# Another written order for the pairs of a decode step's attention, with another kept unit

## Chip, cores, metric

One core of one Trainium2 chip. The metric is the device time of one launch in microseconds, the median of several runs; a profiled execution of the kernel shows where that time is spent.

## What is computed

Two layers, each an attention block over a cache and a gated feed-forward block, for four batches with one new token each. Both layers use the same weights and the same cache.

```python
B, D = 4, 512; Hq, Hkv, Sk, Dh = 32, 8, 4096, 128
def A(x):                                   # attention over the cache
    q = (x @ wq) as [B, Hq, 1, Dh]; k, v = caches, each repeated 4 times over heads
    p = softmax(q @ k.T * Dh ** -0.5)
    return (p @ v) @ wo
def G(x):                                   # F = 1792
    return (sigmoid(x @ w_gate) * (x @ w_up)) @ w_down
for layer in range(2):
    x = x + A(layernorm(x))
    x = x + G(layernorm(x))
```

All tensors are bf16. One batch and one of the 8 heads of the cache make a *unit*: its K and its V are 4096 x 128 values each, 1 MiB. 64 units for two layers would be 128 MiB.

## The kernel before, in words

**Units and pairs.** Work goes in *pairs* of neighbouring units of one batch and layer. `ORDER` lists them as three digits: layer, batch, pair (pair `k` holds units `2k` and `2k+1`). Pair 132 is layer 1, batch 3, units 4 and 5; the text writes a unit as (layer, batch, unit). Pairs are counted from 0 in the order of the list, so the last is pair 31.

**Slots and kept units.** SBUF holds 12 slots of 1 MiB, and four more once the query weights (`wq`) are used for the last time (`yield_wq`). Each slot takes one unit's K or V. `KEPT` names, for each batch, the units whose K (before the stroke) or V (after it) stays in its slot from layer 0 to layer 1 and is not loaded again: 27 in all, in both versions. The others are loaded once in each layer.

**The stream.** `LOADS` is the order in which SyncE issues all transfers: `k` and `v` take the next unit of `ORDER` that must be loaded, `o`, `g`, `u`, `d` are parts of the weights `wo`, `w_gate`, `w_up`, `w_down`. The text counts its letters from 0 and calls that the *place* of a transfer. After every step, `pump()` issues as many as there are free slots, and never out of order: a `k` or `v` without a slot holds back all that follow. A slot comes free when its user is through: two K at the pair's `z`, a V at its unit's second `a`. SyncE does nothing else, so a transfer is queued behind the wait of the one ahead of it. The very last V is cut in two transfers of 512 KiB.

**The program.** `PROGRAM` is one letter per step; each step issues its instructions to the engines, which work through them in order and wait for each other by semaphores. For the n-th pair:
- `t`, `T`: the transpose of half or the whole of one K in its slot, on VectorE (L1018); only for K that are loaded in that layer
- `b`: the pair's queries into blocks, on GpSimd (L732, four copies)
- `s`, `z`: first and second half of the scores, 8 matmuls each (L1035)
- `m`, `p`, `n`: maximum on VectorE (L1053), spread by TensorE (L1061), bias on VectorE (L1072)
- `e`: exponential on ScalarE (L1084)
- `P`, `C`, `D`: the probabilities turned by TensorE (L1106, 9 matmuls) and copied back in two parts of four copies, mostly on ScalarE (L1158)
- `h`, `r`, `i`: the row sums, on GpSimd, TensorE (L1172) and VectorE (L1184)
- `a`: a quarter of the pair's value products, 16 matmuls (L1204); two `a` for each unit
- `o`: normalise on VectorE (L1235); `N` the same for one unit at the very end
- `w`: output rows of a pair whose units are ready (L1260 or L1300), or nothing if none are. In layer 1 a unit is ready only when all four batches are through with it.
- `f`, `F`, `l`: the layer-0 output of a batch turned back into columns
- `x`: sums of the output weights, on ScalarE
- `.`: the next of the 17 steps of a batch's *pass* (`pass_steps`): feed-forward of layer 0 and the queries of layer 1 for that batch. Among them are the gate and up products (L837, L862; L875 combines them on VectorE), their turn (L887, L897), the down product (L957, L972), the layernorm (L494, L581 on TensorE) and the four query products (L908), after which L940, L706 and L717 bring the queries to where `b` reads them. Pairs of layer 1 of a batch can start only after its pass. The last of batch 3's query products is what frees the four `wq` slots.

`s12` in the text is the step `s` of pair 12, `a50` the two `a` steps of the 50th unit in the order of the list (units 2g and 2g+1 are those of pair g).

After the last `a`, the feed-forward block of layer 1 for all four batches and the output follow (L1300 to L1532).

Of the kernel before, what the change touches and what calls it, by code (L numbers as in the profile page):

```python
# [120 lines left out]

KEPT = ["012345/23", "0145/45", "167/067", "014567/7"]
ORDER = """
000 003 002 001 011 013 101 010 012 100 102 021 022 020 023 112 110 111 031 103 123 032 030 033 120
122 121 131 113 132 133 130
"""
LOADS = """
kvkkkkkkvo koovoovkko ovovgvkkvg uuddvvvkkv kkvvkkvvvk kvvvkkvvkk vvvvvvkkvk kvvvkkvvkv kvkkvvkkvv  # L130
kvvkkkvkkk kvkvvvvvvv vvvvv
"""
PROGRAM = """
szmbpTneTh szTTmprPnbDCwiaa swewazaohtPbtrmptCnDtwiaewaa szTbhraPTw
szwmpwonemCiDharpnabawaoPwiDeCTawtPaftFaal sowzmh.p.Dw..r.n.ehwiCP.r...aa..w.awao.Ci.Daa..b
szwTtmptabneaohx sPrzmwpiCDnTaeaaaPobChDriTaax szaawmwbpnx sehzPotrmpibx szCnwDeaatbT
smzpwbafnPahFlCDoeriwma.paT.hTrw..n..Paa seh.zC.Doi.aa.aram..w.oPb.wiDTT.pwCaa
snzm.aaehorPCpnTTwwebD.Pi shaazraaCmpnob sDzeibaaPh
szmrapaoCwnDewbmiahfFaPpaalCorDinweaaaTwTahPCroDi. szm.wbapnTTeaww..hPr..aa
swzboCDia.a.mpn.aaeho.rPiT..DTC...aa sz.a.bmap snezPChwmptrDnoitaabTePwaaohr  # L140
sCizDmaapaanteotwPhrwCiaTbDa szmawpnehbTaroiPTwCDaa szmaapbnoehwfrTPC
szwiDmaaFpanablePhoriCtwtD.aaT..T. sz..maa.pT.b.n soe.zmh..T...wPpCri..abTDna szTePaTbhaw
smrowpziCbnaDameph snPzabeCaorm sDipaPaahDnazrCwbeomwPhCip
sawnaerazamhoDPiwaCraapnaoiwaDaaeaPohCrDiwaaaNwa
"""


def bass_interleave_layers__gqa_block_cached__glu_gated_glu__decode_kernel(
# [147 lines left out]
    pos = {t: i for i, t in enumerate(seq)}  # L296
    hold = [dict(zip("kv", ([int(c) for c in part] for part in text.split("/")))) for text in KEPT]

# [1285 lines left out]
```

## Time and profile before

| | |
|---|---|
| median of 3 runs | 315.44 us (314.36 to 315.73) |
| profiled execution: its time, its span | 315.29 us, 313.2 us |
| TensorE matmuls busy | 228.6 us (73% of the span) |
| VectorE, ScalarE, GpSimd busy | 177.7, 106.7, 40.4 us |
| moved by DMA | 120.45 MB, 385 GB/s in the mean |
| mean granted TensorE clock | 0.719 |

The span runs from the first to the last instruction of the kernel; the execution's own time lies 2.1 us above it. Busy time is the union of an engine's instructions. The profile also holds the chain of work that ended last, followed back from the last instruction (each piece with its start and length in us, and either the engine and line that worked or the DMA that was waited for), and the landing of each transfer, which is when the last of the 16 DMA engines has finished its share.

### The profile page before, as it was taken

To read this page: it belongs to the slowest core of one execution; us is meant where nothing else is said; L and a number is where in the kernel's file an instruction comes from. 1 tells how busy PE (TensorE), PEld (TensorE's weight loads), DVE (VectorE), ACT (ScalarE), POOL (GpSimd) and SP (SyncE) were. 2 spreads that over 40 slices of the span, in tenths; PEclk is the share of its full clock that TensorE was granted. 3 is DMA by queue.
4 is the path that set the end of the run, shared out by engine and by line. 5 is a ranking of instruction groups with operands and counts; after the bars stand their busy time and mean duration, and the time that the engine had idled before them with its cause. 6 is when DMAs were issued, how large, how long until landed. Compare 5 with 4: busy or idle time off the path is not lost.

```text
span 313.2 us, 10155 instructions
## 1 busy us (share of the span) xinstructions
PE 228.6 (73%) x4306; PEld 140.0 (45%) x4306; DVE 177.7 (57%) x396; ACT 106.7 (34%) x351; POOL 40.4 (13%) x205
## 2 busy tenths in 40 slices
PE   1213264562888979798789899978676888799876
PEld 1211042232454354655445747345443543446765
DVE  6344916715424568567742675856655787832243
ACT  2001033043123366343425533344334312457420
POOL 0002110110000213201212011020121010232000
PEclk9999999999999976875655557555555576555555
DMA  7999999999999999999999999999999999999900
GB/s 289 420 426 422 399 375 414 384 422 417 404 417 421 395 374 425 422 422 416 419 392 370 421 425 416 420 421 421 416 419 358 398 365 365 421 426 419 396 31 5
DMA packets 20788, 120.45 MB, mean 385 GB/s; under 512 B 1924, under 2 KB 6024, under 8 KB 7688
## 3 DMA queue, kind: packets, MB, share of 16 engines
q1 hardware_dynamic: 20720, 119.81, 94.2%
q8 instruction: 34, 0.56, 0.7%
q14 instruction: 10, 0.08, 0.1%
q10 hardware_dynamic: 24, 0.01, 0.0%
HBM read 119.80 MB, written 0.00 MB: 383 GB/s over the span
## 4 chain that ended last, share of the span: by engine, by line
PE 37%; DMA 27%; SPq 13%; DVE 11%; ACT 5%; issue 4%; POOL 1%; DVEq 0%; ACTq 0%; POOLq 0%
DMA slot<-in_A_k_cache_dram 13%; PE S_ps L1035 12%; DMA slot<-in_A_v_cache_dram 11%; PE O_ps L1204 9%; SPq L369 8%; DVE slot L1018 7%; SPq L349 5%; PE PT L1106 4%; ACT pT L1158 3%; DMA wq<-in_A_v_cache_dram 3%; PE M_ps L908 2%; PE O_ps L1300 2%; POOL qz L732 1%; ACT pe L1084 1%; DVE small L1053 1%
## 5 line engine op out<-in xcount | busy, mean ns | idle before, releaser
L1018 DVE STREAM_TRANSPOSE slot<-slot 128x2048 f32<-128x2048 f32 (+1 forms) x53 | 103.9, 1973 | 18.9 <-DMA slot<-in_A_k_cache_dram 18.8
L1158 ACT ACTIVATE pT<-PT 32x128 bf16<-32x128 f32 x232 | 62.0, 267 | 69.3 <-PE PT L1106 38.0
L1204 PE MATMUL O_ps<-pT,slot 128*128 128x4 bf16 x1760 | 57.0, 166 | 24.6 <-ACT pT L1158 13.7
L1204 PEld LDWEIGHTS O_ps<-pT,slot 128*128 128x128 bf16 x1760 | 52.9, 103 | 46.0 <-ACT pT L1158 22.6
L1035 PE MATMUL S_ps<-slot,qz 128*16 128x512 bf16 x512 | 59.1, 590 | 15.2 <-DVE slot L1018 8.7
L732 POOL COPY qz<-qs 32x32 bf16<-32x32 bf16 x128 | 26.0, 203 | 125.9 <-PE S_ps L1035 72.5
L1084 ACT ACTIVATE pe<-S_ps,small 128x512 bf16<-128x512 f32 x32 | 22.0, 687 | 57.8 <-DVE small L1072 25.6
L1053 DVE TENSOR_REDUCE small<-S_ps 128x1 bf16<-128x512 f32 x32 | 21.9, 686 | 31.6 <-PE S_ps L1035 31.6
L1106 PE MATMUL PT<-ident_bf,pe 128*128 128x64 bf16 (+1 forms) x288 | 27.7, 235 | 2.7 <-ACT pT L1158 1.3
L1106 PEld LDWEIGHTS PT<-ident_bf,pe 128*128 128x128 bf16 (+1 forms) x288 | 20.4, 123 | 15.9 <-ACT pe L1084 4.3
L1035 PEld LDWEIGHTS S_ps<-slot,qz 128*16 128x16 bf16 x512 | 10.8, 101 | 30.0 <-issue 11.0
L1235 DVE TENSOR_TENSOR oT<-O_ps,small 128x8 bf16<-128x8 f32 (+1 forms) x32 | 5.4, 168 | 26.8 <-PE O_ps L1204 25.5
L1117 POOL CAST small<-small 128x1 bf16<-128x1 f32 x32 | 5.9, 186 | 88.7 <-ACT pe L1084 68.9
L1072 DVE CUSTOM_DVE_ANT_0 O_ps<-O_ps,small 128x64 f32<-128x64 f32 x32 | 9.1, 283 | 14.2 <-PE O_ps L1061 12.2
L908 PE MATMUL M_ps<-wq,small 128*1 128x512 bf16 x128 | 14.1, 605 | 0.0
L1260 PE MATMUL AC<-wo,oT 128*1 128x512 bf16 x96 | 12.5, 599 | 1.4 <-issue 0.8
L1061 PE MATMUL O_ps<-valid_p,small 128*128 128x64 bf16 x32 | 7.2, 225 | 7.5 <-DVE small L1053 6.9
L717 ACT ACTIVATE qs<-M_ps 128x128 bf16<-128x128 f32 x8 | 1.9, 280 | 25.0 <-PE M_ps L706 24.9
L1061 PEld LDWEIGHTS O_ps<-valid_p,small 128*128 128x128 bf16 x32 | 3.3, 103 | 14.5 <-DVE small L1053 11.6
L1300 PE MATMUL O_ps<-oT,wo 128*128 128x1 bf16 (+1 forms) x256 | 8.3, 166 | 1.9 <-issue 1.2
L1172 PE MATMUL O_ps<-small 128*128 128x8 bf16 x62 | 6.4, 174 | 4.2 <-POOL small L1120 3.7
L1172 PEld LDWEIGHTS O_ps<-small 128*128 128x128 bf16 x62 | 4.3, 110 | 11.0 <-issue 4.2
(129 smaller groups left out, 198.3 us busy)
## 6 DMA issues: line engine op xcount, KB each, us to landing
slot<-in_A_v_cache_dram SPq DMA_DIRECT2D x49, 1024.0 KB, 12.2
slot<-in_A_k_cache_dram SPq DMA_DIRECT2D x45, 1024.0 KB, 11.4
wq<-in_A_v_cache_dram SPq DMA_DIRECT2D x6, 1024.0 KB, 13.2
wq<-in_A_wq_dram SPq DMA_DIRECT2D x2, 2048.0 KB, 10.0
wo<-in_A_wo_dram SPq DMA_DIRECT2D x8, 512.0 KB, 14.9
wg<-in_B_w_gate_dram SPq DMA_DIRECT2D x2, 896.0 KB, 15.7
wu<-in_B_w_up_dram SPq DMA_DIRECT2D x2, 896.0 KB, 20.9
wd<-in_B_w_down_dram SPq DMA_DIRECT2D x1, 1024.0 KB, 23.9
```

The lines of the kernel that those rows point to most:

```text
L349: S.dma("sp", (lambda dst, src: lambda e: e.dma_start(dst, src))(dst, src), f"wo{n}" if kind == "wo" else kind, writes=[f"{kind}{n}"])
L369: "sp", (lambda dst, frm: lambda e: e.dma_start(dst, frm))(dst, frm), sem, writes=[key], deps=deps
L732: (lambda a, ps: lambda e: e.tensor_copy(qz_sb[ps, :, :, a, :], qs_sb[b][ps, :, u * REP:(u + 2) * REP].rearrange("p t (u r) -> p u t r", r ...
L908: (lambda k, st: lambda e: e.matmul(M_ps[h][32 * st:32 * st + 1, :], lhsT=xc_bf[:, k, 0:1], rhs=wv[:, k, h, :, st, :], start=(k == 0), sto ...
L1018: dve(lambda e: e.transpose(kf, kf), writes=[f"s{st}"])
L1035: (lambda t, b2, e_, c, r0, ul: lambda e: e.matmul(S_ps[p][r0:r0 + 4 * REP, :], lhsT=qz_sb[:, ul, t, :, :].rearrange("p a r -> p (a r)"), ...
L1053: dve(lambda e: e.tensor_reduce(rm_bf, S_ps[p][:, :], AX.X, ALU.max), reads=[f"S{p}"], writes=["rmb"])
L1084: lambda e: e.activation(pe_sb.rearrange("p j m -> p (j m)"), S_ps[p][:, :], ACTF.Exp, bias=nm_sb, scale=exp_scale, accum_out=sm_sb,),
L1106: (lambda q0, q1, c0, m0, m1, a0, a1: lambda e: e.matmul(PT[q0:q1, c0:c0 + 16 * (a1 - a0)], lhsT=pe_flat[:, m0:m1], rhs=valid_bf[:, :, 4 * ...
L1158: (lambda dst, frm: lambda e: e.activation(dst, frm, ACTF.Copy))(dst, frm),
L1204: (lambda n, x, c, j: lambda e: e.matmul(bank[:, ul * REP:(ul + 1) * REP], lhsT=vv[:, x * JG + c * 4 + j, :], rhs=pT[:, x % 2, j, x // 2, ...
L1300: (lambda c, r: lambda e: e.matmul(out_w[:, c * nb:(c + 1) * nb], lhsT=wo_sb[:, us[0] * REP + r, cols(c)], rhs=oT_sb[:, us[0] * REP + r, c ...
```

## The change

The four strings are replaced; no function is touched.

- `KEPT`: of batch 3, K of units 1, 4, 5, 6, 7 and V of units 6, 7 stay for layer 1, instead of K of units 0, 1, 4, 5, 6, 7 and V of unit 7. Batches 0 to 2 keep the same.
- `ORDER`: layer 0 begins with pair 003 instead of 000, and pairs within the middle change places. The last eight pairs were 120, 122, 121, 131, 113, 132, 133, 130 and need 2, 4, 4, 4, 4, 2, 1, 2 transfers; now they are 120, 121, 111, 133, 131, 130, 122, 132 and need 2, 4, 4, 0, 4, 3, 4, 2. The last unit to be loaded is (1,3,5) instead of (1,3,1).
- `LOADS` and `PROGRAM` follow that order, with the same steps at partly other places.

```diff
-KEPT = ["012345/23", "0145/45", "167/067", "014567/7"]
+KEPT = ["012345/23", "0145/45", "167/067", "14567/67"]
 ORDER = """
-000 003 002 001 011 013 101 010 012 100 102 021 022 020 023 112 110 111 031 103 123 032 030 033 120
-122 121 131 113 132 133 130
+003 002 000 001 011 013 101 010 012 102 100 021 022 020 023 112 110 103 031 113 123 030 032 033 120
+121 111 133 131 130 122 132
 """
 LOADS = """
-kvkkkkkkvo koovoovkko ovovgvkkvg uuddvvvkkv kkvvkkvvvk kvvvkkvvkk vvvvvvkkvk kvvvkkvvkv kvkkvvkkvv
-kvvkkkvkkk kvkvvvvvvv vvvvv
+kkvvkkokok kkkvvokoog oovovkkvvg uuddvvvkkv kkvvkkvvvv kkvkvkvvkk vvvvvvkkvv kkvkvkvvkk vvkkvvkkvv
+kvvkkkvkvv kvkkvkkvvv vvvvv
 """
 PROGRAM = """
...
-swzboCDia.a.mpn.aaeho.rPiT..DTC...aa sz.a.bmap snezPChwmptrDnoitaabTePwaaohr
-sCizDmaapaanteotwPhrwCiaTbDa szmawpnehbTaroiPTwCDaa szmaapbnoehwfrTPC
-szwiDmaaFpanablePhoriCtwtD.aaT..T. sz..maa.pT.b.n soe.zmh..T...wPpCri..abTDna szTePaTbhaw
-smrowpziCbnaDameph snPzabeCaorm sDipaPaahDnazrCwbeomwPhCip
-sawnaerazamhoDPiwaCraapnaoiwaDaaeaPohCrDiwaaaNwa
...
+sDiFlCzampaawbnaeoPthwrit.wCaDTa...Tw swzmb..aap..nTe.oPC shzri.Dwaawm.....pnw.waaTehr.bPCot
+sitzDabmapne sTzhaabmrpowPwniDC sezaaThwwTaarPDbCmo spzneimhbwapPwDanaa
+sCrozeihmPDapCnaaaeowrPiDwChwaaaaawroaiaNwa
 """
```

The text names three steps of these strings often: `a50` and `a51` (in the program before, the value products of units (1,2,4) and (1,2,5); after, of (1,2,2) and (1,2,3)), and the last query product of batch 3, the fifteenth `.` of that batch.

More of the change, by code (lines that the diff above doesn't have):

```diff
@@ L114 @@
 NSLOT = 12
-KEPT = ["012345/23", "0145/45", "167/067", "014567/7"]
+KEPT = ["012345/23", "0145/45", "167/067", "14567/67"]
 ORDER = """
-000 003 002 001 011 013 101 010 012 100 102 021 022 020 023 112 110 111 031 103 123 032 030 033 120
-122 121 131 113 132 133 130
+003 002 000 001 011 013 101 010 012 102 100 021 022 020 023 112 110 103 031 113 123 030 032 033 120
+121 111 133 131 130 122 132
 """
 LOADS = """
-kvkkkkkkvo koovoovkko ovovgvkkvg uuddvvvkkv kkvvkkvvvk kvvvkkvvkk vvvvvvkkvk kvvvkkvvkv kvkkvvkkvv
-kvvkkkvkkk kvkvvvvvvv vvvvv
+kkvvkkokok kkkvvokoog oovovkkvvg uuddvvvkkv kkvvkkvvvv kkvkvkvvkk vvvvvvkkvv kkvkvkvvkk vvkkvvkkvv
+kvvkkkvkvv kvkkvkkvvv vvvvv
 """
 PROGRAM = """
[L134 to L139, printed above, removed]
-swzboCDia.a.mpn.aaeho.rPiT..DTC...aa sz.a.bmap snezPChwmptrDnoitaabTePwaaohr
-sCizDmaapaanteotwPhrwCiaTbDa szmawpnehbTaroiPTwCDaa szmaapbnoehwfrTPC
-szwiDmaaFpanablePhoriCtwtD.aaT..T. sz..maa.pT.b.n soe.zmh..T...wPpCri..abTDna szTePaTbhaw
-smrowpziCbnaDameph snPzabeCaorm sDipaPaahDnazrCwbeomwPhCip
-sawnaerazamhoDPiwaCraapnaoiwaDaaeaPohCrDiwaaaNwa
+sTzmpnbewT szhmPrbTpwTnCi sewzDhampraaaoPTnibeCDTa saaaPhzbTmT sCropnezwwmiaDaTaawpwPbnhworehCDTw
+siPaazmrapfaFlonweC..wD.ih...P.r...aa...aao.Ci.Daa..bTw szmpnaTbehaoPtCrx sizmDapantaaebPThDowrwCx
+siaazbaampx snwezthPmworbpCtx snizwTabwDmewafw sFpnzaawhmoPCDrilw.aa.aaehTo..PrT.bDp.in
+szCe.aaw.ht.Pt.aaoCmrD.iTb..p.naea szam.pahorTnPD.TCwbe.Pihr saazaambCp sznoDebimaa
+szhPbaparnCowwDmiaaePfhaaCDrpneoiaFhaTaarlTPwoi sCzm.Dwaap.anTa..eT.b.hoP
+sCrzbwiamD.ap.neT.aa.ohPT..wD.r sziC..wama.apw.bwta snteTzhPrCbo
+simDzbpanaamaehpPrnDoiCaeahPraaTTCoi szmpanDaebharPawowwCiDaTwaT szbmaapneowhrPTf
+sDiFlCzampaawbnaeoPthwrit.wCaDTa...Tw swzmb..aap..nTe.oPC shzri.Dwaawm.....pnw.waaTehr.bPCot
+sitzDabmapne sTzhaabmrpowPwniDC sezaaThwwTaarPDbCmo spzneimhbwapPwDanaa
+sCrozeihmPDapCnaaaeowrPiDwChwaaaaawroaiaNwa
 """
```

## Prediction

> **What bounds the kernel now.** I read the page first (slices and chain), then the chain of waits in order of time for its last third, then stretches of 2 us, the timeline and SyncE's issues for the end. The slices:
>
> ```profile
> PE   1213264562888979798789899978676888799876
> DMA  7999999999999999999999999999999999999900
> GB/s 289 420 426 422 399 375 414 384 422 417 404 417 421 395 374 425 422 422 416 419 392 370 421 425 416 420 421 421 416 419 358 398 365 365 421 426 419 396 31 5
> ```
>
> The transfers run from the start to slice 38 at 420 GB/s where they are fed, and TensorE is nearly full from slice 13 on. The stream sets the pace; where its rate dips (slices 31 to 34, 235 to 266 us) it is TensorE that is late in freeing slots. From one transfer to the next the trace's landings stand 2.48 us apart (1 MiB, 423 GB/s). The last stage in the chain:
>
> ```profile
> 260.38 3.37 PE M_ps L908 x30
> 263.76 8.07 DMA wq<-in_A_v_cache_dram
> 271.88 1.01 PE O_ps L1204 x32
> ...
> 295.08 0.73 issue
> 295.81 1.85 PE O_ps L1204 x64
> 297.66 0.81 PE PT L1106 x9
> ...
> 299.15 1.16 issue
> 300.31 0.48 PE O_ps L1300 x12
> 300.79 0.87 PE O_ps L1204 x32
> ```
>
> The chain leaves the stream for good at 271.88: the value product of unit (1,2,5) waits for a transfer that could start only at 263.76, when batch 3's last query product (L908) gave the four wq slots free. After it every piece is TensorE's, or a short wait between engines. The stream itself ends earlier:
>
> ```profile
> 296.00:298.00 2.00, 2.00 (x69) 1.95 (x66) 0.18 (x1) 0.00 (x0) 0.00 (x0) 0.50 0.75 297
> 298.00:300.00 2.00, 1.15 (x29) 0.94 (x26) 1.37 (x5) 1.38 (x5) 0.00 (x0) 0.50 0.16 59
> 300.00:302.00 2.00, 1.70 (x60) 1.68 (x60) 0.18 (x2) 0.00 (x0) 0.00 (x0) 0.50 0.04 10
> ```
>
> The DMA share (last but one number) falls from 297 on; by the landings in the trace the two halves of the last V arrive at 299.44 and 300.69. But their products start at 301.50 and 302.78, and the last ends at 303.34; 9.9 us of closing work follow to 313.2. So TensorE ends 2.1 us behind the stream. That is all that the tail can give if the stream stays as it is.
>
> **How the sum stands.** The profiled execution took 315.29 us, 2.1 over its span of 313.2; the median of the three runs is 315.44. I work on the span and carry the difference. 0.5% of it, 1.6 us, is about what a measurement of this kernel can tell from no change.
>
> **What is equal.** Counting the strings, both versions move 115 pieces (101 of K and V, 14 of weights), the same bytes, and issue the same groups on TensorE. One K more is loaded in layer 1 and one V less: one more transpose on VectorE (L1018, 1.97 us in the mean). It lies beside TensorE's last pairs, where VectorE waits (3.44 us of idle before 280.05, 2.97 before 290.48): nothing; if that cover is gone, the maximum (L1053) behind it comes up to 2.3 us late.
>
> **The start.** The first pair is now 003, whose K are places 0 and 1 of LOADS, not 0 and 2: they land at 18.39 instead of 21.93, so scores begin 3.5 us sooner. The chain to 100 us hangs on place 28 (`62.02 16.65 DMA slot<-in_A_v_cache_dram`), the same unit at the same place in both: nothing is gained.
>
> **The middle.** A slot is freed by the second `z` of a K pair or the second `a` of a V. I laid place by place the release in both programs against the TensorE work done before it (groups by their rows: a half of scores 0.97, transposes L1106 0.85, a half of a value product 0.48, output rows 0.95). Most stand within 1 us. One is worse: place 41 is released by z6 one group later (1.0 us); it landed at 109.75, 5.5 us after its issue and with no gap, so it has no slack, and the stream may slip by 1.0; places 44 and 45, where the stream lost 1.3 us, come 1.0 earlier and take it back. Bounds -0.5 to +1.0, taken 0. The loss at place 64 (2.2 us) stays: it hangs on value products of the same transfers, 60 and 61. Places 88 to 94 come 1.9 to 4.0 us of work sooner, but the stream is full there (9 us from issue to landing), and place 90, which starts pair 120, keeps its place: taken 0, bounds -1.5 (the whole lag that its landing shows, 3.99 us instead of 2.48) to 0.
>
> **The tail.** Releases by place, from the strings:
>
> | places | before | after |
> |---|---|---|
> | 95, 96 | z24, a46 | z24, z24 |
> | 97; 98, 99; 100 | a48; z25; a49 | the same |
> | 101, 102 | z26 | z26 |
> | 103 | last query product | a50 |
> | 104 to 106 | last query product | the same |
> | 107 | a50 | last query product |
> | 108 to 114 | z27, z27, a51, z28, z28, a52, z29 | a51, z27, z27, a52, z28, z28, a53 |
>
> (1) Pair 25's transposes, sums and first value product (0.83 + 0.15 + 0.94 = 1.9 us) now stand ahead of batch 3's last query products, and its maximum ahead of L875 on VectorE (0.3 late, of the 0.69 that it takes): the last query product ends at 263.7 + 1.9 + 0.3 = 265.9. On SyncE the four transfers behind it, and all that is queued after them, go out 2.2 later. (2) The stream: 101 and 102 leave 0.3 later (269.7 for the landing of 102), 103 lands at 272.2, and 104, out at 266, follows without a gap. Eleven more at 2.48 end at 299.5; with the lag of 1.55 that the last six transfers of before show, 301.1, against 300.69. (3) TensorE's work from there to the last value product: 34.5 us before, 32.6 after. Its waits were 39.6 - 34.5 = 5.1. The 1.2 before 271.88 and about 1 before 267.0 go, since the V wanted there are now places 98 and 99, landed by 261. What is late next: the query chain (L940, L706, L717, L732) has less work beside it, 1.2; the maximum of pair 133 stands on VectorE behind two half transposes of place 102 (269.7 + 2.5, then 0.7), 0.4 more than the value products cover; pair 131's exponential stands on ScalarE behind eight copies of pair 133 (L1158, 8 x 0.28), 0.9, and L1106 and the next scores queue behind it. At the end before has 2.4 (0.73, 1.16 and two short ones), and I take 1.5: the 1.16 has no releaser, and may fall elsewhere or not at all (bounds 0.3 and 2.6). Sum 4.0. Last product: 265.9 + 32.6 + 4.0 = 302.5, against 303.34: 0.9 sooner, and behind the stream (301.1 + 0.5), which thus doesn't bind. The closing work is the same.
>
> 315.29 - 0.9 = **314.4 us**; its bounds -1.5 to +1.5 from the terms above, so 313.2 to 316.0 for this case alone.
>
> For a transfer into a dry queue, 5.5 us is the shortest row. [...]
>
> **Rivals.**
> *Faster: the stream ends it (0.33).* If the waits of the end don't come back and the last landing's lag is 0.3 instead of 1.55, the last product starts at 299.9 and the time is 315.29 - 2.9 = 312.4; with place 90's lag gone too, 311. For it: every V of the last pairs is wanted 1 to 4 us of work later than that of the same place before; against it: TensorE must do its 32.6 us with under 2 us of waits, and did not before.
> *Slower: batch 3's pass is late (0.24).* VectorE is full at 252 to 256 us, and each step of the pass (L875, L897, L972) needs it in turn. Now the maximum of pair 25 goes ahead of L875 (0.7), and a transpose of K (1,1,3) (2.3) ahead of L972. If both hold the pass up in full, its end is 3.0 later, and all pairs of batch 3 with it: 314.4 + 3.0 = 317.4. It decides if the last L908 ends after 268.
> *The slow stream (0.02).* If the last eleven transfers ran at the 365 GB/s of slices 33 and 34 (2.87 each), they would end at 272.2 + 31.6 + 1.55 = 305.4, and the time would be 318. In those slices a transfer went out 2 to 6 us before the one ahead of it landed; here it is over 6. [...]
> *It doesn't do what it says (0.03).* New waits eat all that the old ones give: 315.3.
>
> **Numbers.** Forecast 0.38: same 0.31, faster 0.04, slower 0.03. First rival 0.33 faster; second 0.24 and third 0.02 slower; fourth same 0.02, slower 0.01. Faster 0.37, same 0.33, slower 0.30. Range: first rival less 1.0, second plus 0.6: 311.4 to 318.0; it leaves out the ends of both and the third, about 0.15.
>
> **What would show it.** Right: no wait for a transfer before L1204 after 262; the last L908 at 265.9; four wq issues at 266; the last landing near 301 and the last L1204 near 302.5. Wrong: L908 past 268 (second rival), L1204 ending right on the last landing before 300.5 (first), or a span that is longer already where pair 120's scores begin (239.4).

## The result, and the profile after

| | before | after |
|---|---|---|
| median of 17 runs each, in turn on one chip | 314.40 us (313.27 to 316.38) | 313.48 us (312.30 to 314.13) |
| profiled execution: its time, its span | 315.29, 313.2 us | 312.81, 310.6 us |
| from the start of pair 24's scores to the last query product's end | 24.32 us | 25.94 us |
| from there to the last value product's end | 39.63 us | 36.08 us |
| closing work | 9.86 us | 10.44 us |

The ratio after to before is 0.9956, 95% interval 0.9938 to 0.9974. By the medians that is 0.9 us less, as forecast; by the means, and so by the ratio, it is 1.4 us. Both lie within the 0.5% that the prediction called about what can be told from no change. That outcome had a chance of 0.33; "faster", with 0.37, had been given more. Two repeats on other chips gave 0.9961 (0.9939 to 0.9982) and 0.9968 (0.9949 to 0.9986). The two profiled executions lie 2.5 us apart, because that of before was 0.9 above its median and that of after 0.7 below; a single pair of profiles would have told too much.

The slices of after, from the page; TensorE, the DMA share and the rate:

```profile
PE   1232366244889789799879898986768989789975
DMA  7999999999999999999999999999999999999900
GB/s 290 417 424 411 407 422 378 390 406 419 407 415 418 413 379 415 426 418 418 419 390 386 424 421 420 421 419 419 420 414 424 400 358 401 424 422 420 407 27 5
```

The stream runs at the same rate to the same slice, and the dip where TensorE is late in freeing slots is three slices long (32 to 34: 400, 358 and 401 GB/s) instead of four. TensorE stays nearly full behind it. The chain of waits of after, around the last query product and at the end (start and length in us):

```profile
260.65 3.47 PE M_ps L907 x31
264.28 0.58 issue
264.87 0.28 DVE O_ps L1071
265.29 0.79 ACT pe L1083 x2
...
267.55 0.21 POOL qz L731
267.81 0.20 POOL qz L731
268.07 0.20 POOL qz L731
268.33 0.22 POOL qz L731
268.60 1.89 PE S_ps L1034 x15
...
278.33 1.87 PE O_ps L1203 x64
...
294.77 1.44 PE O_ps L1203 x54
296.21 1.30 issue
297.51 0.83 PE O_ps L1203 x26
```

(All lines of after stand one lower than before's.) Where before had 8.07 us of waiting for a transfer behind the query product (L908, now L907), the chain has the engines' own work: the queries' way through GpSimd (L731), scores, value products. The waits of TensorE from 262 us to the last value product, first before, then after (us in total, times, longest):

```profile
PE O_ps L1204 <- DMA wq<-in_A_v_cache_dram: 1.2, 1, 1.2
PE O_ps L1300 <- issue: 1.2, 1, 1.2
PE O_ps L1204 <- ACT pT L1158: 1.1, 1, 1.1
PE O_ps L1300 <- DVE oT L1235: 0.7, 2, 0.5
PE O_ps L1204 <- issue: 0.7, 1, 0.7
PE M_ps L940 <- ACT pT L1158: 0.4, 1, 0.4
PE M_ps L706 <- DVE t_row L946: 0.4, 1, 0.4
PE S_ps L1035 <- ACT slot L1158: 0.2, 1, 0.2
PE S_ps L1035 <- POOL qz L732: 0.2, 1, 0.2
```

```profile
PE O_ps L1203 <- issue: 1.3, 1, 1.3
PE M_ps L939 <- issue: 0.8, 1, 0.8
PE S_ps L1034 <- POOL qz L731: 0.7, 1, 0.7
PE O_ps L1203 <- ACT pT L1157: 0.7, 1, 0.7
PE O_ps L1171 <- POOL small L1119: 0.5, 1, 0.5
PE O_ps L1299 <- DVE oT L1234: 0.3, 1, 0.3
PE O_ps L1060 <- DVE small L1052: 0.3, 1, 0.3
```

The wait for a transfer (1.2) and the one for copies behind the query product (1.1) are gone. The query chain takes more (0.8 at L939 and 0.7 at L1034, against 0.4, 0.4 and 0.2 in before), and a wait for row sums on GpSimd (L1119, 0.5) is new. No value product waits for a transfer any more. The pause with no releaser is in both, at the end, 1.2 and 1.3.

### The profile page after: what moved, and what is told of

The parts are those of the page before. It is cut to its first block, busy times and chain, and to the rows that moved or that the text cites. A ratio compares the mean times of both kernels' runs of the same rounds, so it can differ in the third digit from the quotient of the medians.

```text
span 310.6 us, 10146 instructions
## 1 busy us (share of the span) xinstructions
PE 227.0 (73%) x4306; PEld 138.5 (45%) x4306; DVE 179.8 (58%) x395; ACT 106.8 (34%) x351; POOL 40.4 (13%) x205
## 4 chain that ended last, share of the span: by engine, by line
PE 26%; DMA 16%; DVE 9%; issue 4%; ACT 4%; POOL 1%; DVEq 0%; ACTq 0%; POOLq 0%; SPq 0%
DMA slot<-in_A_k_cache_dram 9%; PE O_ps L1203 8%; DMA slot<-in_A_v_cache_dram 7%; PE S_ps L1034 6%; DVE slot L1017 6%; PE PT L1105 3%; ACT pT L1157 3%; PE O_ps L1299 2%; PE M_ps L907 1%; POOL qz L731 1%; ACT pe L1083 1%; DVE small L1052 1%; PE O_ps L1060 1%; PE AC L1259 1%; PE M_ps L956 1%
## 5 line engine op out<-in xcount | busy, mean ns | idle before, releaser
L1017 DVE STREAM_TRANSPOSE slot<-slot 128x2048 f32<-128x2048 f32 (+1 forms) x50 | 101.5, 2040 | 24.5 <-DMA slot<-in_A_k_cache_dram 24.5
L1157 ACT ACTIVATE pT<-PT 32x128 bf16<-32x128 f32 x236 | 63.1, 267 | 58.6 <-PE PT L1105 38.6
L1034 PE MATMUL S_ps<-slot,qz 128*16 128x512 bf16 x496 | 56.6, 586 | 22.0 <-DVE slot L1017 10.9
L1203 PEld LDWEIGHTS O_ps<-pT,slot 128*128 128x128 bf16 x1856 | 54.8, 103 | 32.0 <-ACT pT L1157 19.2
L1203 PE MATMUL O_ps<-pT,slot 128*128 128x4 bf16 x1856 | 58.2, 166 | 12.3 <-ACT pT L1157 7.2
L731 POOL COPY qz<-qs 32x32 bf16<-32x32 bf16 x128 | 26.0, 203 | 106.2 <-PE S_ps L1034 62.8
L1052 DVE TENSOR_REDUCE small<-S_ps 128x1 bf16<-128x512 f32 x32 | 21.9, 684 | 29.1 <-PE S_ps L1034 28.8
L1034 PEld LDWEIGHTS S_ps<-slot,qz 128*16 128x16 bf16 x496 | 10.6, 102 | 40.6 <-DVE slot L1017 13.2
L907 PE MATMUL M_ps<-wq,small 128*1 128x512 bf16 x128 | 14.6, 604 | 0.0
```

The lines of the kernel that those rows point to most:

```text
L731: (lambda a, ps: lambda e: e.tensor_copy(qz_sb[ps, :, :, a, :], qs_sb[b][ps, :, u * REP:(u + 2) * REP].rearrange("p t (u r) -> p u t r", r ...
L907: (lambda k, st: lambda e: e.matmul(M_ps[h][32 * st:32 * st + 1, :], lhsT=xc_bf[:, k, 0:1], rhs=wv[:, k, h, :, st, :], start=(k == 0), sto ...
L1017: dve(lambda e: e.transpose(kf, kf), writes=[f"s{st}"])
L1034: (lambda t, b2, e_, c, r0, ul: lambda e: e.matmul(S_ps[p][r0:r0 + 4 * REP, :], lhsT=qz_sb[:, ul, t, :, :].rearrange("p a r -> p (a r)"), ...
L1052: dve(lambda e: e.tensor_reduce(rm_bf, S_ps[p][:, :], AX.X, ALU.max), reads=[f"S{p}"], writes=["rmb"])
L1157: (lambda dst, frm: lambda e: e.activation(dst, frm, ACTF.Copy))(dst, frm),
```

## Experiments

Each is compared in turn with before on one chip; the first three share a chip, the next four another, the last four a third. All figures are medians, and ratios are to before with their 95% interval.

**1. Which half of the lists makes the gain.** The lists were cut in two at one point: KEPT is of after's or before's tail, the rest changes at letter 98 of LOADS and at pair 24's exponential in PROGRAM.

```diff
 h1: before's lists to the cut, after's from it
-ORDER ... 112 110 111 031 103 ... 120 122 121 131 113 132 133 130
+ORDER ... 112 110 113 031 103 ... 120 121 111 133 131 130 122 132
 h2: after's lists to the cut, before's from it
-ORDER ... 110 103 031 113 123 ... 120 121 111 133 131 130 122 132
+ORDER ... 110 103 031 111 123 ... 120 122 121 131 113 132 133 130
```

> The front of before (up to and with the exponential of pair 24, and LOADS up to place 96), the tail, the kept units and the last pairs of after; pairs 111 and 113 change places so that every pair occurs once. Theory (the gain is made in the tail): 0.9 us faster than before, ratio 0.997, and the stretch from pair 24's first scores (239.4 in before, 238.1 in after) to the end of the last value product is 62 us as in after, not 64 as in before. Rival (the gain is made ahead of pair 24, by the other start and the earlier releases of places 88 to 94): as before, ratio 1.000, with pair 24's scores beginning at 239 to 240.

> The mirror of the first: the front of after, with the tail, the kept units and the last pairs of before. Theory (the gain is made in the tail): as before, ratio 1.000 with 0.3% either way, stretch from pair 24's scores to the last value product 64 us. Rival (the gain is made in the front): 0.9 to 1.4 us faster than before, ratio 0.996, pair 24's scores beginning at 238.

> The changed kernel once more, for a second profile and its ratio on the chip of the two mixed ones. If the 1.3 us by which pair 24's scores began sooner in its first profile belong to the change, they are there again (238.1); if they were the lag of one transfer in one execution, they may be gone (239 to 240) and the time still 0.9 us under before. Theory: ratio 0.996, the wait for a V before L1203 after 262 us absent again, the last query product within 0.7 of 264.1 minus what pair 24's start moves.

Measured: h1 312.82 us, 0.9944 (0.9924 to 0.9964); h2 314.53 us, 1.0003 (0.998 to 1.0026); after 313.34 us, 0.9961 (0.9939 to 0.9982); before 314.43. The whole gain is made behind the cut, and the front, with another first pair and another order in the middle, gives nothing that these runs can tell. In the profiles the stretch from pair 24's scores to the last value product is 62.40 us in h1 and 62.80 in the repeat of after, 64.11 in h2, against 62.03 and 63.95 in the first pair. When pair 24's scores begin differs from execution to execution: 238.1 to 239.4 over these five, and with after's own lists 238.1, 239.2 and 238.1. Over all twelve executions in this document without added instructions the mean is 239.1 with before's front (five) and 238.5 with after's (seven). So about half of the 1.3 us that after was ahead there in its first profile is the chance of one execution; a rest of 0.6 may be the front's, but h2's times show no gain from it.

**2. Is the end TensorE's or the stream's?** One V less is loaded: the V of unit (1,3,0), the last but one, or that of (1,2,5), which before waits for at 271.88; in after, the last but one, (1,3,4).

```diff
+            if kind == "v" and n == 62:      # 51 in the second
+                where["v", b, u] = s
+                continue
```

> The kernel before without the transfer at place 113 (V of unit (1,3,0)); the product reads what the slot held, so that unit's values are not the reference's. Place 114 then lands 2.5 us sooner (298.2 instead of 300.7 in the profile). Theory (before, TensorE ends behind the stream): at most 0.5 us, ratio 0.998 to 1.000, the last value product still near 303. Rival (the last landing sets the end): 2.5 us, ratio 0.992.

> The kernel before without the transfer at place 103 (V of unit (1,2,5)), the one that the product at 271.88 waited for; that unit's values are not the reference's. All later places land 2.5 us sooner. Theory (that wait was TensorE's loss): the idle 1.2 us before that product is gone, its value product ends 1.0 to 1.2 us sooner after pair 24's start, and the time falls by 0.6 to 1.2 us (ratio 0.996 to 0.998), more than without place 113. Rival (the wait covers others that end as late, above all ScalarE's copies and VectorE's transposes): the time stays, ratio 0.999 to 1.001.

> The kernel after without the transfer at place 113 (V of unit (1,3,4)); that unit's values are not the reference's. Theory (TensorE still ends it: its last product began 1.6 us behind the landing): 0 to 0.5 us, ratio to before 0.995 to 0.996. Rival (the stream now binds, as the change wants): 1.5 to 2.5 us faster than after, ratio to before 0.988 to 0.991.

Measured: before without the last but one 313.06 us, 0.9965 (0.9942 to 0.9988); without the middle one 312.64, 0.9956 (0.9936 to 0.9977); after without the last but one 311.87, 0.9923 (0.9897 to 0.9949); before 314.31. The first gained 1.2 us where at most 0.5 was expected, though no value product of the end had waited for a transfer. The second gained 1.7 us where 0.6 to 1.2 was expected, and the third lies between its two forecasts. The chain of waits of the first shows why:

```profile
295.23 1.71 PE O_ps L1207 x64
296.94 0.81 PE PT L1109 x9
297.90 0.85 PE O_ps L1303 x32
298.75 0.43 PE O_ps L1207 x16
299.20 0.58 PE O_ps L1207 x16
```

In before a pause of 1.16 us without a releaser stood inside the output products (L1300 there, L1303 here). Here it is gone, and in the other two as well. So the end hung on the stream after all, by way of that pause rather than of a V that was late. (In the second kernel the wait for a transfer, 1.2 us in before's profile, is gone too, so its gain has two sources.) Experiment 4 takes it up.

**3. What the earlier query work costs.** In after, pair 25's query work (`P`, `C`, `r`, `i`, `D`) and its first value product go back behind the last query product.

```diff
-nTe.oPC shzri.Dwaawm.....pnw.waaTehr.b
+nTe.o shz.wwm.....PpCrinw.DaawaaTehr.b
```

> The kernel after with pair 25's transposes, copies, sums and first value product (P, C, r, i, D and both a of its first unit) put back behind batch 3's last query product, as in before. My step (1) says that product ends 1.9 us sooner (from pair 24's first scores 24.0 us instead of 25.9) and the same work comes back behind it: no change of the time, ratio to before 0.995 to 0.997. Rival (the work filled idle stretches of the pass, so moving it back costs): 0.5 to 1.5 us slower than after, ratio to before 0.998 to 1.001.

Measured: 313.86 us, 0.9994 (0.9973 to 1.0015); before 314.31. Its profile, in the timeline of TensorE (start, length, line; in brackets the idle time before and its releaser):

```profile
257.33 1.89 PE L1033 MATMUL S_ps<-slot,qz 128*16 128x512 bf16 x16 [0.80 <-DVE slot L1016]
259.14 0.59 PE L492 MATMUL M_ps<-small 128*128 128x4 f32 x2
260.39 0.59 PE L579 MATMUL M_ps<-t_row,small 128*128 128x4 f32 x2 [0.66 <-DVE t_row L528]
```

From pair 24's scores to the last query product it takes 25.65 us, only 0.3 less than after: with the query work gone, TensorE waits for VectorE there (0.80 and 0.66). Put ahead, most of the work had filled idle time. Behind the query product the waits for ScalarE's copies (L1156 here) come to 2.0 us, where after (L1157) has 0.7.

A second time, beside after and h1 on one chip:

> After, with pair 25's query work and its first value product put back behind the last query product, a second time, on one chip with after itself. Its first runs gave a ratio to before of 0.9994 (0.9973 to 1.0015), after's gave 0.9956 and 0.9961 on other chips. Theory by its profile (the moved work filled stretches in which TensorE waited for VectorE, so moving it back frees little ahead of the last query product and adds its time behind it): slower than after by 0.5 to 1.2 us, ratio to before 0.998 to 1.000. Rival (the first difference was chance): within 0.4 us of after, ratio 0.995 to 0.997. The prediction's own step (the move costs 1.9 us ahead of the last query product and takes as much away behind it) also says within 0.4 us of after.

> After, unchanged, on one chip with the three others, to compare them with. 313.4 us, ratio to before 0.994 to 0.998. The pause before the 3,997th product is there again, 0.9 to 1.9 us long.

> The front of before with the tail of after, a second time, on one chip with after itself: its first ratio to before was 0.9944 (0.9924 to 0.9964), the fastest that kept all the work. If the front of after costs something, it is 0.3 to 0.6 us faster than after here; if the gain is the tail's alone and the front is neutral, the two agree within 0.3 us.

Measured: 313.68 us, 0.9971 (0.9954 to 0.9988) for the query work put back; 313.44, 0.9968 (0.9949 to 0.9986) for after; 312.72, 0.9938 (0.9916 to 0.996) for h1; before 314.57. On one chip the query work put back costs 0.2 us, which 12 runs each can't tell from nothing. What the order of these steps is worth isn't settled, though. By the ratios, both runs of it together lie some 0.6 us above the three of after, with an interval from 0 to 1.1. And in the profiles the stretch from pair 24's scores to the last value product, without the pause of experiment 4, is 62.5 and 62.4 us with the work put back, against 60.7 to 61.8 in the three of after and 62.8 in before. h1 was ahead of after by 0.5 and 0.7 us on the two chips, with intervals that overlap each time. It is the best order that was run with all its work, and a hint that after's front costs about half a microsecond; that is not settled.

**4. The pause at the end.** In nine of the ten executions with all transfers the pause comes before the 8,130th or 8,131st TensorE instruction, weight loads and the engine's semaphore instructions counted, whatever work stands there: inside output products at L1300 in before, inside value products at L1203 in after. It ends 1.3 to 1.5 us after a transfer of 16 KB in the queue of instructions. To move the instructions against the work, 64 small products, which nothing reads, were put far ahead.

```diff
     q_spread(0, Bn)
+    S.group("pe", [lambda e: e.matmul(AC[:, 0:Bn], lhsT=ident_bf[:, :],
+        rhs=ident_bf[:, 0:Bn], start=True, stop=True) for _ in range(64)], ...)
     q_blocks(0)
```

> After, with 64 small products (128x128 by 128x4, into an unused sum) put on TensorE behind the first spreading of the queries, far ahead of the tail; they move every later TensorE instruction 128 places down its instruction list, and no result is changed. The profile of after has a pause of 1.30 us without a releaser inside the last value products (ends at 297.51), before its 3,997th matrix product and its 8,130th TensorE instruction, weight loads counted; four other executions have it at the same instruction, 1 to 1.8 us long, behind a 16 KB instruction transfer. Theory (the engine waits there for the next block of its instruction list): in the shifted kernel a pause, where there is one, is again before the 3,997th product, which is now 64 products earlier in the work, in the output product at L1299 that after ran at 294.4 us; none is left before the old work place (the 4,061st product). Rival (the pause belongs to the work, a wait that the profile does not show): it stays at the 4,061st product. Time: the 64 products take some 0.6 to 1.7 us at a stage where TensorE is mostly idle, so 0 to the time before pair 24; end within 0.5 us of after by theory and rival, up to 1.3 faster if the pause falls where TensorE waits anyway.

Measured: 313.73 us, 0.9973 (0.9951 to 0.9995), 0.3 us above after on the same chip and not to be told from it. The timeline of TensorE, first after, then the shifted kernel:

```profile
293.75 1.01 PE L1299 MATMUL O_ps<-oT,wo 128*128 128x4 bf16 x32
294.63 1.58 PE L1203 MATMUL O_ps<-slot,slot 128*128 128x4 bf16 x54
297.51 0.41 PE L1203 MATMUL O_ps<-slot,slot 128*128 128x4 bf16 x10 [1.30 <-issue]
```

```profile
295.61 0.77 PE L1299 MATMUL O_ps<-oT,wo 128*128 128x4 bf16 x23
297.13 0.40 PE L1299 MATMUL O_ps<-oT,wo 128*128 128x4 bf16 x9 [0.75 <-issue]
297.39 1.85 PE L1203 MATMUL O_ps<-slot,slot 128*128 128x4 bf16 x64
```

The pause has moved 63 products up in the work, into the output products, and the 64 value products that held it in after run through: it belongs to the number of the instruction. The rival, a wait of the work itself, falls. A second one of 0.32 us follows 256 instructions later, at 301.04. Not every stretch without a releaser is of this kind: in after's profile one of 1.40 us ends at 230.11 (L1203) and one of 0.83 at 265.05 (L939), and in the shifted kernel they stand before the same work as there (1.38 us at 232.21 and 0.80 at 266.92), 128 instructions further on in the list.

These are all thirteen executions, from the trace: when the instruction 256 places earlier ran, when the 16 KB transfer started and ended, when TensorE reached the place and when it went on.

| kernel | 256 earlier | transfer | reached | went on |
|---|---|---|---|---|
| before | 294.07 | 297.71 to 298.78 | 299.15 | 300.31 |
| after | 292.01 | 294.96 to 296.02 | 296.21 | 297.51 |
| after, second | 294.17 | 296.89 to 297.95 | 298.38 | 299.35 |
| after, third | 292.11 | 295.81 to 296.87 | 296.31 | 298.16 |
| h1 | 292.14 | 295.74 to 296.83 | 296.35 | 298.17 |
| h1, second | 292.74 | 295.89 to 296.95 | 296.95 | 298.31 |
| h2 | 293.56 | 297.39 to 298.45 | 298.25 | 299.84 |
| shifted | 291.64 | 294.72 to 295.79 | 296.38 | 297.13 |
| query work back | 294.48 | 296.22 to 297.28 | no pause | 298.70 |
| the same, second | 293.83 | 297.39 to 298.45 | 298.04 | 299.95 |
| before, last V but one left out | 294.22 | 295.35 to 296.26 | no pause | 298.30 |
| before, middle V left out | 293.38 | 294.50 to 295.43 | no pause | 297.46 |
| after, last V but one left out | 292.56 | 294.26 to 295.18 | no pause | 296.64 |

Wherever the engine paused, it went on 1.3 to 1.5 us after the transfer's end. With all the data on its way the transfer starts 2.7 to 3.8 us after the instruction 256 places earlier, once 1.7; with one V less, 1.1 to 1.7. With 1.06 us for itself and 1.4 behind it, that is over 5 us, against the 4.0 to 4.9 us in which TensorE ran through the 256 instructions before the pause (292.01 to 296.04 in after, from the start of the first to the start of the last). The other places 256 instructions apart agree: from 100 us on, the transfer of after's profile started 2.6 to 6.6 us after its place at the 25 places under the stream, and 1.1 to 1.3 us after it at the three behind the stream's end. The DMA's load alone doesn't set it, though: the other two executions of after have one each under the stream that started after 1.2 and 1.4 us, and the 1.1 us of before without the middle V came with the DMA 0.99 busy in the 2 us ahead.

## Why the prediction was right

**The sum.** Forecast 314.4 us, measured 313.48; the change -0.9 and -0.92 (by the ratio -1.4). It is right in size and by the mechanism named, with terms that erred both ways.

**Start and middle, taken as 0.** Right: h2 has both of them and gives 1.0003. Neither bound came true in a way that could be seen; the first pair's 3.5 us are swallowed later, as argued (place 28 landed at 78.67 in before and at 78.58 in after).

**Step 1, the last query product at 265.9.** 264.08, 265.23 and 264.08 in the three executions of after. From pair 24's scores the term +2.2 was 1.6 to 1.7 (24.32 us before, 25.94 to 26.02 after); h2 alone, with before's tail, took 25.27. The step mis-sized the 1.9 us of moved TensorE work: it was put on the path in full, but by experiment 3 it accounts for only 0.3 to 0.4 us, since without it TensorE waits for VectorE. The other 1.3 stay when the work is put back (25.65 against 24.32), and h2 has 0.9 of them without the new tail; what costs them was not tried. The four transfers into the query weights' slots went out at 264.1 to 266.3 in the first profile, where 266 was forecast. The second rival decided past 268 and was never near.

**Step 2, the stream.** Forecast 301.1 for the last landing; 298.04, 300.08 and 299.53 in the three of after, 300.69 before. Counted from pair 24's scores, 61.7 was forecast and 59.9, 60.9 and 61.5 were measured. The lag of 1.55 us carried over from before's last six transfers is an accident of the execution: behind place 103 the three of after lost 1.2, 0.0 and 1.6 us. In the first profile it fell on place 106 (274.50 to 278.16), and the last six then landed 2.48 us apart (288.10, 290.58, 293.06, 295.56, and the halves at 296.80 and 298.04). Of the 3.1 us by which its stream ended sooner than forecast, 2.7 lie ahead of that row: place 103, forecast to land at 272.2, landed at 269.52, and 1.3 of that is the earlier start of pair 24's scores. In the other two it landed at 272.79 and 270.68. The slow stream didn't come: slices 35 to 37 show 424, 422 and 420 GB/s. Two transfers into a nearly empty queue took 5.2 and 5.6 us from issue to landing (250.66 to 255.88, 258.60 to 264.20), about the 5.5 of before's shortest row. So "the stream doesn't bind" held for the data: the last value product ends 2.1 us behind the last landing (300.17), and 2.65 in before (303.34).

**Step 3, work and waits.** TensorE's busy time from the last query product to the last value product fell from 33.52 to 31.31 us, -2.2 where -1.9 was forecast. Its waits went from 6.1 to 4.8, -1.3 where -1.1 was forecast (5.1 to 4.0; both ends were taken 0.8 to 1.0 too low, because the work, added up from rows to 34.5 and 32.6 us, was taken 1.0 and 1.3 too high, and the waits of before are what was left of the stretch). By terms: the transfer's wait and the one before 267 are gone (1.2, 1.1); in two other executions with before's tail (h2, and before without the last V but one) the first was only 0.4 and 0.5, so 1.2 is the high end of that term. The query chain came to 1.5, not 1.2, and the wait for row sums (0.5) was not foreseen. The maximum (L1052) came to 0.3, not 0.4. ScalarE's copies came to 0.7, not 0.9, with another waiter than named: the value products wait for the eight copies, and the exponential behind them hinders nobody. The end came to 1.6, not 1.5.

So in the first pair of profiles the stretch from pair 24's scores is +1.6 - 2.2 - 1.3 = -1.9; 1.3 more is when that stretch began, which experiment 1 puts down to the execution at least in half, and 0.6 was lost in the closing work. Of these three the medians keep 0.9 and the means 1.4. Which of the waits that went makes how much of it isn't shown: the runs place the gain in the tail, and the profiles show these waits gone.

**The closing work, taken as the same.** 10.44 instead of 9.86 in the first profile, 9.89 and 9.91 in the other two: same. The 0.6 of the first holds a pause of 0.37 us at 305.68 without a releaser, 513 instructions behind the first one.

**The rivals.** The stream didn't end it, batch 3's pass was not late, and the change does what it says: h2, without the new tail, is level with before.

**"TensorE ends behind the stream, and that is all that the tail can give."** Half right. No data was late, but leaving out one V gave 1.2 and 1.7 us in before, and by the ratios 1.0 to 1.4 in after, and the pause was gone each time. So the length of the stream does count at the end, through the pause, which stood in the prediction's sum as a term without a cause. The prediction had bounds of 0.3 to 2.6 for the waits of the end and wrote that the 1.16 "has no releaser, and may fall elsewhere or not at all". It was the right caution: over ten executions with all transfers the pause measured 1.16, 1.30, 0.97, 1.85, 1.82, 1.36, 1.59, 0.75, next to nothing and 1.91 us, mostly more than the whole change.

## What to carry to other kernels

Work moved ahead of a critical chain may fit into that chain's own waits for another engine: here 1.9 us of work made it 0.3 longer, and without that work TensorE waited 0.80 and 0.66 us for VectorE. So look for these waits first. When an idle stretch has no releaser, count the engine's instructions to its place and move them against the work: here the one at the end kept its number while 63 products went past it, so it was no wait of the work, and two others (1.40 and 0.83 us in after) moved along with the work. Compare stretches between marks in the program over several executions, since here the start of one stretch alone strayed by more than the change was worth (238.1 to 239.4 us, against 0.9).

## What was not expected of the hardware

In this kernel TensorE paused at a fixed number of its instruction list, among short instructions (256 in 4.0 to 4.9 us) at the end of a full stream of transfers: 0.75 to 1.91 us in nine of ten executions with all transfers, none in three with one less. Others stand at multiples of 256 instructions from it (in before also 4,608 instructions earlier, ending at 154.78, 0.79 us, and 5,376 earlier, ending at 131.94, 0.98 us, and in the two of before with one V less 512 later, 0.64 and 0.51 us), and each ends behind a 16 KB transfer of the queue of instructions (the two earlier ones of before 1.27 and 1.37 us behind it):

```profile
q8 instruction: 34, 0.56, 0.7%
```

That is one transfer of 16 KB for every 258 instructions of TensorE: before's trace has 8,758 (4,306 products, as many weight loads, and 146 that do no work of their own, mostly for semaphores). The shifted kernel shows that the pause goes with the number of the instruction: it moved 63 products up in the work when 64 were put ahead. That the engine waits there for the next block of its list is the author's reading, from this and from the 1.3 to 1.5 us between a transfer's end and the end of the pause. That the block comes late because its transfer queues behind the data is what the table speaks for (2.7 to 3.8 us, once 1.7, after the instruction 256 places earlier with all the data, 1.1 to 1.7 with one V less), and the times at the other places; no run slowed the data down alone, so what exactly it waits for stays open. Most of the 28 places 256 instructions apart show no pause: after's profile has one of over 0.25 us at two of them (1.30 us here, 0.37 at 305.68), that of before at three (0.98, 0.79 and 1.16). At this one 256 instructions last 4.0 to 4.9 us, and in nine of ten executions TensorE went on 5.2 to 6.3 us after the instruction 256 places earlier; in the tenth, without a pause, it took 4.2.
